# Weight splitting one attention step later, and attention's loads ahead of the weight pieces, in a fused attention and expert-layer kernel

## The chip, the cores and the metric

The kernel runs on one core of a Trainium2 chip. The metric is the device time of one execution in microseconds (us). The core has TensorE (PE, with its weight loads as PEld), VectorE (DVE), ScalarE (ACT), GpSimd (POOL) and SyncE (SP), which here only issues DMAs. Each engine runs its instructions in the order of the program; they meet through semaphores.

## What is computed

The reference runs three layers one after the other. The first is an attention over 2 batches and 8 heads of size 64: 512 local queries see the keys within 32 places of their own and 32 global keys, and 32 global queries see all 544 keys. Its 1088 rows of 512 go through a dense layer with a squared relu (512 to 2048 to 512), and then through a layer of 8 experts, where each row takes one expert.

```python
s_ll = np.where(np.abs(pos[:, None] - pos[None, :]) <= 32, scale * q_l @ k_l.T, -1e9)
a_l = sm(np.concatenate([scale * q_l @ k_g.T, s_ll], axis=-1))
out_l = a_l @ np.concatenate([v_g, v_l], axis=2)
out_g = sm(scale * q_g @ k_all.T) @ v_all
x = concatenate([out_g, out_l], axis=2)          # rows of 512
x = np.square(np.maximum(x @ w_in, 0)) @ w_out   # moe_
# moe2_: expert e = argmax(x @ w_gate); out = gate * relu(x @ w1[e]) @ w2[e]
```

## The kernel before

**Attention** is a loop over steps u (line 248). A step handles half of a pair of heads: n = u // 2 is the pair (8 of them in the two batches), and 16 steps have scores; the loop runs on for a few more steps to drain its pipeline. What a step does, and in which order, stands in the string `ORDER`: `S0` and `S1` are the scores of the step's first and second two blocks (TensorE L123, VectorE L127 for mask and row minimum, ScalarE L130 for the exponential), `N` normalizes the step before (VectorE L134 and L135, GpSimd L138 and L140), `T` transposes the probabilities of two steps ago (TensorE L147 and L151, copied out by VectorE at L148 and by ScalarE at L152), `V0` and `V1` multiply the probabilities of three steps ago with the values (TensorE L165 and, for the global values, L168), `X` copies the result (ScalarE L175). Every fourth step also has the global queries: `GS` their scores (L186, L189), `GX` their maximum and exponential (VectorE L197 to L199, ScalarE L200 and L201), and in the three steps behind it `GN`, `GT` and `GV` (L206 to L234). Score tiles have two PSUM buffers (L60), which the global scores' second part uses too.

**Weights.** The next layer multiplies float32 numbers as sums of a high and a low part. `Weights` (line 283) makes these from pieces of 1 MB: `prefetch` loads a piece by DMA (L315) into one of three stage buffers, `queue` turns it into five steps, `last` (VectorE L359), `sign` (L364), `rebase` (ScalarE L367), `clamp` (VectorE L372) and `join` (L375), and the piece's end, `high` (ScalarE L336), `low` (VectorE L339) and the next `prefetch`, is hung on to steps of the piece behind it. `run(n)` issues the next n steps. The loop's places `f0` to `f4` call it: `EARLY[u][part]` is how many steps the place runs. The same places run the splits of x near the end of the loop (L511, L514).

**Loads.** `START` lists what is loaded ahead of the loop, `NEXT[n]` what is issued at `L` in the odd step of pair n, in this order, all on SP's queue: `k` keys and queries (L74, L75), `v` values (L80), `h` global values (L88), `g` global queries (L84), `w` pieces of weights (L315). SP runs them one behind the other, each with its waits: for its buffer, and for the load eight places earlier, whose semaphore it takes over. Keys have four buffers, queries three, values four, global queries one.

```python
for what in ORDER.split():
    if what == "S0" and u < NU: scores(u); scores_h(u, 0)
    ...
    elif what == "L" and hf == LH and n < len(NEXT):
        begin(NEXT[n])
    elif what[0] == "f":
        filler(u, int(what[1:]))      # W.run(EARLY[u][part])
```

Behind the loop come the dense layer (`moe1`: L533 to L535 and L553 to L555, with the rest of the weight steps among its matmuls) and the experts (`moe2`).

Of the kernel before, what the change touches and what calls it, by code (L numbers as in the profile page):

```python
# [22 lines left out]
LP, LV, GT, GV = 2, 3, 1, 2  # L23
NP, NPT = 3, 3
NS, CUT, NK, NQ, NV = 2, (0, 2, 4, 8), 4, 3, 4
START = "k1 v0 h w1 g0"
NEXT = ["w1 k2 v1", "w1 k3 v2", "k4 v3", "k5 v4 h0 h1", "k6 v5 g1 h2", "k7 v6 h3", "v7"]
LH = 1

SPLIT = [s for u in (16, 17, 18, 19) for s in ((u, 4), (u + 1, 2))]  # L30

EARLY = [[0] * 5] * 2 + [[1, 0, 1, 0, 0]] * 12 + [[0, 0, 1, 0, 0]] * 4 + [[0] * 5] * 4
RATE = [[2, 2]] * 8 + [[2, 3]] * 4 + [[0, 0]] * 4
RATE2 = [[0, 0]] * 8 + [[2, 3], [2, 2]] * 4
NST = 3
# [10 lines left out]
def attention(tc, ctx, ident, x, qb_d, kd_d, vw_d, qg_d, vg_d, filler):  # L46
# [175 lines left out]
    def g_pv(g):  # L222
        b = g // 2
        d = gs.pop(("t", g))
        o = ps_o.tile([128, 4, 64], F32, name="og", tag="o")
        for j in range(2):
            v = ld["v", 2 * g + j]
            for c in range(5):
                k, w = (slice(0, 128), 2 * c) if c < 4 else (slice(64, 96), 7)
                for h in range(2):  # L230
                    p, q = slice(64 * h, 64 * h + 64), slice(64 * j + 32 * h, 64 * j + 32 * h + 32)
                    nc.tensor.matmul(o[p, j, 0:32], lhsT=v[k, w, p], rhs=d[k, c, q], start=(c == 0), stop=(c == 4))
        hp0 = 2 * g % 4
        nc.vector.tensor_copy(x[:, hp0:hp0 + 2, b * ST:b * ST + SG], o[:, 0:2, 0:32])  # L234

    def begin(what):
        for w in what.split():
            if w[0] == "w":
                filler(-1, int(w[1:]))
            elif w == "h":  # L240
                load_vg(0, slice(0, 512))
            elif w[0] == "h":
                load_vg(1, slice(128 * int(w[1:]), 128 * int(w[1:]) + 128))
            else:
                {"k": load, "v": load_v, "g": load_g}[w[0]](int(w[1:]))

    begin(START)
    for u in range(NU + LV + 2):
        n, hf = divmod(u, 2)
        g, r = divmod(u, 4)  # L250
        for what in ORDER.split():
# [23 lines left out]
            elif what == "GV" and r == GV and 0 < g <= 4:  # L275
                g_pv(g - 1)
# [3 lines that stand above are left out]
# [125 lines left out]
def attention_moe_kernel(ctx, tc, qb, kd, vw, qg, vg, w_in, w_out, w_gate, w_gate_t, w1, w2, capacity, out):  # L405
# [24 lines left out]
    def filler(u, part):  # L430
        if u < 0:
            W.prefetch(part)
        else:
            W.run(EARLY[u][part])
        for v, p in SPLIT:
# [684 lines left out]
```

## Time and profile before

| | |
|---|---|
| time, median of 3 runs (lowest to highest) | 462.59 us (462.2 to 468.64) |
| the profiled execution: its time, its span | 462.7 us, 461.0 us |
| PE busy | 432.4 us (94%) |
| DVE, ACT, POOL busy | 315.8 us (69%), 249.1 us (54%), 79.4 us (17%) |
| mean granted clock of PE | 0.988 |
| moved by DMA | 77.26 MB, mean 168 GB/s |
| attention's loop | up to 85.56 us, the first matmul of the dense layer |

The span runs from the first to the last instruction. A row of a timeline has the start in us, the length, the engine, the line, what is written and read, and in brackets how long the engine had been idle before it and what ended that. A row of a wait has the total, how many times, and the longest. The granted clock of 1.00 is 2.4 GHz, 0.50 is 1.2 GHz. A matmul of float32 numbers is two instructions in the rows.

### The profile page before, as it was taken

The numbers are of one execution on the slowest core, as the hardware profiler recorded it, in microseconds if no ns is written. First come the engines' busy times: TensorE is split into PE (matmuls) and PEld (weight loads), VectorE is DVE, ScalarE is ACT, GpSimd is POOL, SyncE is SP. The second block draws the span as 40 slices with busy tenths as digits, with TensorE's granted clock in tenths as the row PEclk, the third lists the DMA queues.
The fourth block names the chain that finished last, engine by engine and source line by source line (L and its number), as shares of the span: only waits on it lengthen the run. The fifth ranks groups of instructions, "written<-read, shape, count | busy, mean of one in ns | idle before, by whom it ended". The sixth has DMA issues, their size and how long they took to land. (4 is left out here: it accounts for less than half of the span.)

```text
span 461.0 us, 8010 instructions
## 1 busy us (share of the span) xinstructions
PE 432.4 (94%) x2963; PEld 368.8 (80%) x2963; DVE 315.8 (69%) x690; ACT 249.1 (54%) x488; POOL 79.4 (17%) x106
## 2 busy tenths in 40 slices
PE   5799999999999999999999999799999999999992
PEld 4677777888887889899999999677787777877970
DVE  3598987588799627974598688466974888647200
ACT  4587876576777734222533393156755777356210
POOL 3265636000000000000000000403202512051010
PEclk9899999999999999999999999899999999999998
DMA  8958952325254421005010468485992899711010
GB/s 250 399 182 316 326 196 94 96 91 182 97 186 176 169 104 48 24 1 194 25 46 1 146 254 332 122 257 208 306 305 95 309 349 366 298 52 41 1 39 21
DMA packets 24601, 77.26 MB, mean 168 GB/s; under 512 B 3689, under 2 KB 4841, under 8 KB 24288
## 3 DMA queue, kind: packets, MB, share of 16 engines
q1 hardware_dynamic: 19456, 64.38, 38.7%
q0 software_dynamic: 2384, 6.78, 4.9%
q10 hardware_dynamic: 2704, 5.37, 3.2%
q8 instruction: 32, 0.52, 0.5%
q14 instruction: 25, 0.20, 0.1%
HBM read 70.08 MB, written 7.41 MB: 168 GB/s over the span
## 5 line engine op out<-in xcount | busy, mean ns | idle before, releaser
L339 DVE TENSOR_TENSOR wlo<-ws,whi 128x1024 fp32r<-128x1024 f32 x80 | 94.6, 1219 | 11.5 <-ACT whi L336 10.5
L336 ACT CAST whi<-ws 128x1024 fp32r<-128x1024 f32 x80 | 83.0, 1075 | 19.2 <-DVE ws L375 10.3
L554 PE MATMUL y<-gl,whi 128*128 128x512 f32 (+2 forms) x192 | 63.2, 329 | 1.6 <-DVE gl L545 1.6
L533 PE MATMUL h<-xh,whi 128*128 128x512 f32 (+2 forms) x192 | 63.8, 332 | 0.6 <-ACT r L539 0.6
L535 PE MATMUL h<-xh,wlo 128*128 128x512 f32 (+2 forms) x192 | 62.9, 328 | 0.2 <-DVE wlo L339 0.2
L553 PE MATMUL y<-gh,whi 128*128 128x512 f32 (+2 forms) x192 | 62.9, 327 | 0.0
L534 PE MATMUL h<-xl,whi 128*128 128x512 f32 (+2 forms) x192 | 62.8, 327 | 0.0
L555 PE MATMUL y<-gh,wlo 128*128 128x512 f32 (+2 forms) x192 | 62.8, 327 | 0.0
L539 ACT ACTIVATE r<-h 128x512 f32<-128x512 f32 (+2 forms) x48 | 22.5, 470 | 42.8 <-PE h L535 35.7
L554 PEld LDWEIGHTS y<-gl,whi 128*128 128x128 f32 x192 | 36.3, 189 | 4.8 <-DVE gl L545 2.3
L533 PEld LDWEIGHTS h<-xh,whi 128*128 128x128 f32 x192 | 36.3, 189 | 3.4 <-ACT r L539 0.9
L535 PEld LDWEIGHTS h<-xh,wlo 128*128 128x128 f32 x192 | 36.3, 189 | 3.1 <-DVE wlo L339 0.6
L534 PEld LDWEIGHTS h<-xl,whi 128*128 128x128 f32 x192 | 36.3, 189 | 2.5
L545 DVE TENSOR_TENSOR gl<-r,gh 128x512 fp32r<-128x512 f32 (+2 forms) x48 | 25.7, 536 | 18.4 <-ACT r L542 15.5
L553 PEld LDWEIGHTS y<-gh,whi 128*128 128x128 f32 x192 | 36.3, 189 | 2.5
L555 PEld LDWEIGHTS y<-gh,wlo 128*128 128x128 f32 x192 | 36.3, 189 | 2.5
L130 ACT ACTIVATE P<-P,mn 128x160 f32<-128x160 f32 x64 | 27.0, 427 | 16.4 <-DVE mn L127 14.1
L583 DVE CUSTOM_DVE_ANT_0 junk<-yr,ws 128x512 bf16<-128x512 f32 x48 | 33.1, 690 | 1.2
L123 PE MATMUL s<-kd,qb 128*128 128x160 f32 x128 | 26.7, 343 | 5.2 <-DMA qb<-qb 5.2
L904 PE MATMUL bank_o<-whi,hh 128*128 128x512 f32 x72 | 29.9, 415 | 0.0
L870 POOL DMA_INDIRECT out_dram<-os,sidx x11 | 12.6, 1145 | 97.1 <-ACT os L866 96.5
L905 PE MATMUL bank_o<-wlo,hh 128*128 128x512 f32 x72 | 28.3, 393 | 0.0
(205 smaller groups left out, 895.0 us busy)
## 6 DMA issues: line engine op xcount, KB each, us to landing
ws<-w SPq DMA_DIRECT2D x62, 512.0 KB
ws<-w_in SPq DMA_DIRECT2D x8, 1024.0 KB
ws<-w_out SPq DMA_DIRECT2D x8, 1024.0 KB
vw<-vw SPq DMA_DIRECT2D x8, 512.0 KB
qb<-qb SPq DMA_DIRECT2D x7, 512.0 KB
kd<-kd SPq DMA_DIRECT2D x7, 416.0 KB
ws<-w_gate_t SPq DMA_DIRECT2D x2, 1024.0 KB
out_dram<-yr ACTq DMA_DIRECT2D x1, 2048.0 KB
```

What stands on the lines that cost most here:

```text
L130: nc.scalar.activation(out=P[:, a], in_=P[:, a], func=AF.Exp, bias=mn[:, a:a + 1], scale=-1.0, accum_out=su[:, a:a + 1])
L336: self.nc.scalar.copy(d["h"], f)
L339: self.nc.vector.tensor_tensor(out=d["l"], in0=f, in1=d["h"].bitcast(F32), op=ALU.subtract)
L533: nc.tensor.matmul(h, lhsT=whi[:, k, fs], rhs=xh[k], start=(k == 0), stop=False)
L534: nc.tensor.matmul(h, lhsT=whi[:, k, fs], rhs=xl[k], start=False, stop=False)
L535: nc.tensor.matmul(h, lhsT=wlo[:, k, fs], rhs=xh[k], start=False, stop=(k == 3))
L553: nc.tensor.matmul(ys[d][:, 0:gh.shape[1]], lhsT=whi[:, f % 4, ds_], rhs=gh, start=(f == 0), stop=False)
L554: nc.tensor.matmul(ys[d][:, 0:gh.shape[1]], lhsT=whi[:, f % 4, ds_], rhs=gl, start=False, stop=False)
L555: nc.tensor.matmul(ys[d][:, 0:gh.shape[1]], lhsT=wlo[:, f % 4, ds_], rhs=gh, start=False, stop=(f == 15))
L583: nc.vector.tensor_tensor_reduce(out=junk, in0=yr, in1=wgb[e], scale=1.0, scalar=0.0, op0=ALU.mult, op1=ALU.add, accum_out=L[:, i, e:e + 1])
L904: nc.tensor.matmul(o, lhsT=hh[:, k], rhs=wh[:, k % 4], start=(k == 0), stop=False)
L905: nc.tensor.matmul(o, lhsT=hh[:, k], rhs=wl[:, k % 4], start=False, stop=False)
```

## The change

Three tables of numbers and words are changed, no function.

```diff
-START = "k1 v0 h w1 g0"
-NEXT = ["w1 k2 v1", "w1 k3 v2", "k4 v3", "k5 v4 h0 h1", "k6 v5 g1 h2", "k7 v6 h3", "v7"]
+START = "k1 v0 h g0 w1"
+NEXT = ["k2 v1 w1", "k3 v2 w1", "k4 v3", "g1 k5 v4 h0 h1", "k6 v5 h2", "k7 v6 h3", "v7"]
-EARLY = [[0] * 5] * 2 + [[1, 0, 1, 0, 0]] * 12 + [[0, 0, 1, 0, 0]] * 4 + [[0] * 5] * 4
+EARLY = [[0] * 5] * 3 + [[1, 0, 1, 0, 0]] * 12 + [[0, 0, 1, 0, 0]] * 4 + [[0] * 5] * 3
```

By `EARLY` the weight steps begin in u=3 instead of u=2, and each of the 28 steps of the loop stands one u later. By `START` and `NEXT` the global queries stand ahead of the first piece, the keys, queries and values of pairs 2 and 3 ahead of the second and third piece, and the second batch's global queries are loaded in u=7 instead of u=9.

On VectorE, from the normalization in u=2 on, in the kernel before (`ws` is the piece of weights, `tp` the transposes, `PT` their copy, `P` the probabilities):

```order
L135 RECIPROCAL su<-su 128x4
L359 TENSOR_SCALAR ws<-ws 128x1024
L148 COPY PT<-tp_239 128x128
L127 ISA P,mn<-s,mask 128x160
L127 ISA mn 128x1
...
L364 SCALAR_TENSOR_TENSOR ws<-ws 128x1024
```

and from the same place in the changed one, to the same step of weights:

```order
L135 RECIPROCAL su<-su 128x4
L148 COPY PT<-tp_238 128x128
L127 ISA P,mn<-s,mask 128x160
L127 ISA mn 128x1
...
L135 RECIPROCAL su<-su 128x4
L359 TENSOR_SCALAR ws<-ws 128x1024
L148 COPY PT<-tp_282 128x128
...
L364 SCALAR_TENSOR_TENSOR ws<-ws 128x1024
L197 TENSOR_REDUCE m_306<-sg 128x1
```

The first weight step L359 moved from ahead of the first copy of transposes to ahead of the second one, and L364 to just ahead of the maximum of the first global scores.

On ScalarE, from the exponentials of u=2 and u=3 on, in the kernel before:

```order
L130 ACTIVATE P,su<-P,mn 128x160 x4
L367 ACTIVATE ws<-ws 128x1024
L152 COPY PT<-tp 128x512
L130 ACTIVATE P,su<-P,mn 128x160 x2
L200 ACTIVATE Pg,sg__310<-sg,nbg 128x480
L201 ACTIVATE Pg,sg__310<-sg_303,nbg 128x64
L175 COPY x<-o 128x256
```

and in the changed one:

```order
L130 ACTIVATE P,su<-P,mn 128x160 x4
L152 COPY PT<-tp 128x512
L130 ACTIVATE P,su<-P,mn 128x160 x2
L200 ACTIVATE Pg,sg__308<-sg,nbg 128x480
L201 ACTIVATE Pg,sg__308<-sg_301,nbg 128x64
L175 COPY x<-o 128x256
L130 ACTIVATE P,su<-P,mn 128x160 x2
L367 ACTIVATE ws<-ws 128x1024
L152 COPY PT<-tp 128x512
```

The rescaling L367 moved from ahead of the copy of transposes in u=3 to ahead of the copy in u=4.

On SP, at the beginning of its loads, as one piece of the difference (`kd` keys, `qb` queries, `vw` values, `vgz` global values, `qg` global queries):

```order
 L80 DMA vw<-vw 128x1024
 L88 DMA vgz<-vg 32x512 x4
+L84 DMA qg<-qg 128x512
 L315 DMA ws<-w_in 128x2x1024
-L84 DMA qg<-qg 128x512
+L74 DMA kd<-kd 128x832
+L75 DMA qb<-qb 128x1024
+L80 DMA vw<-vw 128x1024
 L315 DMA ws<-w_in 128x2x1024
 L74 DMA kd<-kd 128x832
```

The global queries moved ahead of the first piece, and the keys, queries and values of pair 2 ahead of the second.

## Rows read from the trace of the kernel before

**Rows 1.** Windows: length; busy us (count) of PE, PEld, DVE, ACT, POOL; PEclk, DMA.

```profile
22.35:40.61 18.26, 17.62 (x238) 14.19 (x234) 16.25 (x61) 14.60 (x48) 11.55 (x12) 1.00 0.70 268
...
85.56:290.00 204.44, 201.41 (x1263) 184.30 (x1259) 155.06 (x328) 102.79 (x175) 0.53 (x1) 1.00 0.34 121
290.00:461.00 171.00, 156.07 (x772) 123.66 (x772) 96.59 (x126) 84.96 (x118) 37.44 (x32) 0.98 0.53 185
```

**Rows 2.** Waits of PE up to 22.35 us: total, times, longest.

```profile
PE o L168 <- DVE PT L148: 2.3, 1, 2.3
```

**Rows 3.** Timeline of DVE, where weight steps begin.

```profile
15.59 0.69 DVE L359 TENSOR_SCALAR ws<-ws 128x1024 int32<-128x1024 int32 x1 [3.22 <-DMA ws<-w_in]
16.20 0.28 DVE L148 COPY PT<-tp 128x128 f32<-128x128 f32 x1
16.41 0.31 DVE L127 CUSTOM_DVE_ANT_0 P<-s,mask 128x160 f32<-128x160 f32 x1
...
16.89 1.22 DVE L364 SCALAR_TENSOR_TENSOR ws<-ws 128x1024 int32<-128x1024 int32 x1
```

**Rows 4.** Timeline of PE: steps 3, 4 and 5, and step 7 into 8.

```profile
13.87 0.34 PE L165 MATMUL o<-PT,vw 128*64 128x64 f32 x4
16.54 0.48 PE L168 MATMUL o<-PT,vgz 128*64 128x64 f32 x4 [2.34 <-DVE PT L148]
...
18.50 1.20 PE L123 MATMUL s<-kd,qb 128*128 128x160 f32 x4
...
22.35 0.81 PE L123 MATMUL s<-kd,qb 128*128 128x160 f32 x4
...
24.31 0.71 PE L123 MATMUL s<-kd,qb 128*128 128x160 f32 x4
...
26.31 0.34 PE L165 MATMUL o<-PT,vw 128*64 128x64 f32 x4
...
36.03 0.34 PE L165 MATMUL o<-PT,vw 128*64 128x64 f32 x4
...
37.24 0.71 PE L123 MATMUL s<-kd,qb 128*128 128x160 f32 x4
...
40.61 0.81 PE L123 MATMUL s<-kd,qb 128*128 128x160 f32 x4
```

**Rows 5.** Windows at the start, columns as in rows 1; the last two: DMA share, GB/s.

```profile
0.00:15.50 15.50, 8.87 (x37) 7.50 (x37) 5.17 (x25) 6.53 (x22) 5.95 (x21) 1.00 0.86 283
...
12.50:14.50 2.00, 1.71 (x14) 1.39 (x13) 0.00 (x0) 0.89 (x3) 1.54 (x3) 1.00 1.02 405
...
16.40:19.50 3.10, 2.96 (x21) 2.84 (x22) 2.63 (x13) 1.99 (x9) 0.47 (x2) 0.50 1.03 411
```

**Rows 6.** The page's DMA issues: what, queue, count, KB each.

```profile
ws<-w_in SPq DMA_DIRECT2D x8, 1024.0 KB
...
qg<-qg SPq DMA_DIRECT2D x2, 256.0 KB
```

**Rows 7.** Timelines of DVE and ACT, steps 3 and 4.

```profile
21.45 0.66 DVE L197 TENSOR_REDUCE m<-sg 128x1 f32<-128x480 f32 x1 [0.31 <-PE sg L186]
...
19.29 1.13 ACT L367 ACTIVATE ws<-ws 128x1024 f32<-128x1024 f32 x1
...
22.59 0.66 ACT L200 ACTIVATE Pg<-sg,nbg 128x480 f32<-128x480 f32 x1 [0.87 <-DVE nbg L199]
...
23.53 0.37 ACT L175 COPY x<-o 128x256 f32<-128x256 f32 x1
...
24.61 0.58 ACT L152 COPY PT<-tp 128x512 f32<-128x512 f32 x1
```

**Rows 8.** Waits of PE from 22.35 to 85.56 us.

```profile
PE tp L151 <- POOL Pw L140: 0.7, 2, 0.4
...
PE sg L186 <- DMA qg<-qg: 0.3, 1, 0.3
```

**Rows 9.** GpSimd's products: ns of one, shortest, median, longest.

```profile
L140 POOL TENSOR_TENSOR Pw<-P,su x32: 607/614/1692, 10.6 to 78.6; 128x256 f32<-128x256 f32 x32
```

## The prediction, made before the changed kernel was run

> **What bounds the kernel now.** I read four views in this order. The windows by stage [rows 1] tell who is full: in the first whole four steps of the attention loop (22.35 to 40.61 us) TensorE is busy 17.62 of 18.26 us and VectorE 16.25; from the dense layer on (85.56 to 290 us) TensorE is busy 201.41 of 204.44 us, in the last stage 156.07 of 171.00. So from 22 us on TensorE sets the pace, and what it gains before is carried to the end, unless it is lost again to a new wait. The waits of TensorE then tell where it stood still before 22 us [rows 2]: apart from the first loads, once, 2.3 us, for the copy at L148. The timeline of VectorE shows why [rows 3]: L359, the first split step of a weight piece, began at 15.59 after 3.22 us of waiting for its DMA, so VectorE had been free since 12.37; L148, which needs nothing of the weights, stood behind it and began at 16.20. TensorE's own timeline [rows 4] shows the hole: L165 at 13.87, L168 only at 16.54. The windows around it [rows 5] add the second half of the price: TensorE's granted clock was 1.00 (2.4 GHz) before the hole, and 0.50 (1.2 GHz) from 16.40 to 19.50 behind it.
>
> **What the change removes.** Steps of attention are called u. In u=2 VectorE no longer meets L359 and L364, so L148 can start at 12.37 and the hole in front of L168 goes. TensorE's work from the first L165 of a step to its second scores takes 1.21 us at full clock (36.03 to 37.24 in step 7), and from there to the next step's first scores, global scores included, 3.37 us (37.24 to 40.61) [rows 4]. So step 3's second scores come at 13.87 + 1.21 = 15.08 (before 18.50), step 4's first scores at 18.45 (before 22.35). Up to here TensorE gains 3.90 us: the hole and the slow clock.
>
> **What it puts in its place: VectorE's chain in step 3.** L359 now stands in step 3, and still waits for the first piece. That piece lies in the queue behind one more load, the global queries, of 256 KB [rows 6]. By 15.50 us the queue had moved 283 GB/s x 15.5 us = 4.4 MB [rows 5], while the loads up to and with the piece are 3.7 MB (416 + 512 KB twice for keys and queries, 512 for values, 256 for global values, 1024 for the piece, by the shapes in the code): so it went nearly in the order of issue, and 262 kB more at 405 GB/s is 0.65 us: landing at 16.24. Bounds: 15.59, if the queries cost nothing; and 15.59 + 0.65 + 3.6 = 19.9, if the piece shares the engines evenly with the keys, queries and values now issued behind it (416 + 512 + 512 KB = 1.47 MB, 3.6 us at 405 GB/s). I take 16.24, since the bytes moved speak for order.
> From there, by starts and durations in rows 3: L359 0.61, L148 0.21, two L127 0.48, L364 1.22: VectorE reaches L197 at 18.76. From L197 to the first exponential of the global scores 1.14 us, and 0.94 to the copy behind the second one (21.45, 22.59, 23.53) [rows 7]: 20.84. Only then is the score buffer free that step 4's second scores take (two buffers, L60). Without that wait they would come at 18.45 + 1.96 (22.35 to 24.31) = 20.41. So TensorE waits 0.43 us and the gain falls to 24.31 - 20.84 = 3.47.
>
> **ScalarE in step 4.** The rescaling L367 (1.13 us) now stands in front of step 4's copy of the transposes (L152), where before it stood in step 3. From the copy L175 to L152 took 1.08 us (23.53 to 24.61), L152 itself 0.58 [rows 7]: 20.84 + 1.08 + 1.13 + 0.58 = 23.63. TensorE needs that copy for step 5's L165, which would otherwise come 2.00 us after step 4's second scores (24.31 to 26.31 [rows 4]), at 22.84. It waits 0.79 us more: the gain falls to 26.31 - 23.63 = 2.68.
>
> **What it gives back later.** Two later waits of TensorE were for things that now come relatively earlier. In step 6 it waited 0.4 us for GpSimd's products L140 [rows 8]; with TensorE 2.7 us earlier and VectorE's sums (L134, L135) earlier by more than that (its chain above runs 3.4 to 4 us ahead of before), this wait goes: +0.4. In step 11 it waited 0.3 us for the second global queries [rows 8], whose load is now issued two steps earlier: +0.3. Sum: 2.68 + 0.4 + 0.3 = **3.4 us**.
>
> **What I cost at nothing.** The rest of the split steps only slide by one step: their number (28 before the dense layer) is the same, and two per step run against every phase of the four-step pattern in turn. The keys and queries of step 4 lie 1 MB earlier in the queue: 4.0 MB before them and 0.95 MB of their own, against 4.4 MB moved by 15.50, so the last byte at about 15.5 + 0.57/0.405 = 16.9 us, 1.5 us ahead of 18.45; the cover is thin, and a microsecond of lateness would be a microsecond of loss. The second load of global queries now waits, at SP, for the global scores of step 7, and the keys and values of step 10 stand behind it: about 37 us, for use about 46 us; nine us for some 2.5 MB. At the end of attention one split step more (L339, 1.2 us) and a rescaling lie among the splits of x; the capacity load behind them is later by about as much. TensorE's next needs there were covered by a few tenths, and I leave that as plus or minus 0.3.
>
> **The sum.** The profiled execution took 462.7 us (span 461.0), by 0.1 above the median of the three runs, 462.59. 462.7 - 3.4 = **459.3 us**.
>
> **The rivals.**
> 1. *A transfer takes the place of the wait.* The piece lands at 19.9, the late bound. VectorE's chain is then 3.7 us later, TensorE stands still in step 4 instead: 3.4 - 3.7 = -0.3, 463.0, no change that can be told; a fall of the clock in that new hole, as in the old one, would be 1.5 more. Against it: the bytes above. The Trainium skill ("DMA: Bandwidth & Descriptors", Queues, rings and completion order) says that completion is not in the order of issue over the 16 engines; by that rule this rival is open, and the 0.7 MB that had moved beyond the piece by 15.50 agree that the order is not strict. Chance 0.12.
> 2. *The clock falls all the same* (TensorE's work in steps 3 and 4 is not enough to hold it): 3.1 us at 0.50 [rows 5] cost half of that, 1.5 us: 460.8. Against it: in the walk above TensorE has no gap from 12.5 to 20.4 us. Chance 0.08.
> 3. *Slower: GpSimd becomes late.* One L140 took 607 to 1692 ns [rows 9], long where VectorE's split steps ran. If, with the steps one place on, the long ones fell into every step, TensorE would wait 0.4 us in each of the 14 steps from 2 to 15: 14 x 0.43 = 6.0 - 3.4 = 2.6 us slower, 465.3. It decides from 0.24 us a step on. Against it: it waited only twice [rows 8], and the products have a whole step (4.6 us, 18.26 / 4) before their transposes. The Trainium skill ("GPSIMD Engine Reference", Specifications) has GpSimd share its SBUF interfaces with VectorE, contended by VectorE instructions with two SBUF inputs; the 607 against 1692 ns agree. Chance 0.04.
> 4. *More gain*: neither the score buffer nor L367 holds TensorE (the piece lands at 15.59, and copies overlap better than in my walk): 3.90 + 0.7 = 4.6 us: 458.1. Chance 0.13.
>
> **How the numbers follow.** The forecast has 0.63, with its own range of 458.6 to 460.3. With rivals 2 and 4 that is 0.84: the range is 457.9 to 461.6, and leaves out rivals 1 and 3. A measurement of this kernel tells about 2% (9.3 us) from no change; the largest gain of any case is 4.6 us, the largest loss 2.6 us, so all of them lie within it: faster 0.01, same 0.98, slower 0.01.
>
> **What the profile of the changed kernel would show.** L148 first at about 12.4 and no wait of TensorE in front of the first L168; the granted clock 1.00 from 12.5 on; VectorE waiting about 1 us at the first L359, at 16.2; TensorE's first scores of step 4 at 18.5, second scores at 20.8 behind the global exponential, L165 of step 5 at 23.6 behind L152; no wait for the global queries in step 11; the first matmul of the dense layer at 85.56 - 3.4 = 82.2 us; stages behind that as long as before. The prediction is wrong if the first L359 begins after 17.2, if TensorE waits for a load of keys or queries after 10 us, or if the loop's four steps take over 18.5 us.

## The result and the profile after

Over 20 runs each, the changed kernel takes 460.45 us (median; 457.87 to 466.71) and the kernel before 464.88 us (462.2 to 469.32). The ratio is 0.9896, with a 95% interval of 0.9868 to 0.9925: a gain of 4.4 us by the medians and of 4.8 by the ratio (3.5 to 6.1), clear of the noise but inside the 2% that count as no change. Medians here are over all runs of a kernel; ratios, intervals and the last column of the table below leave out the few runs more than 1.5% above the kernel's fastest. The profiled execution took 462.06 us, with a span of 460.3 us. A second profile of the same kernel, from a run of its own (`after_again`, below), took 458.71 us, with a span of 457.0.

TensorE's timeline in the changed kernel, from the first L165 of step 3 to step 5 (start, length, engine, line, what; in brackets the idle time before and what ended it); it answers to [rows 4]:

```profile
15.60 0.34 PE L165 MATMUL o<-PT,vw 128*64 128x64 f32 x4
15.77 0.29 PE L168 MATMUL o<-PT,vgz 128*64 128x64 f32 x4
...
16.82 0.71 PE L123 MATMUL s<-kd,qb 128*128 128x160 f32 x4
...
20.18 0.81 PE L123 MATMUL s<-kd,qb 128*128 128x160 f32 x4
...
22.14 0.71 PE L123 MATMUL s<-kd,qb 128*128 128x160 f32 x4
...
24.88 0.34 PE L165 MATMUL o<-PT,vw 128*64 128x64 f32 x4 [0.68 <-ACT PT L152]
```

The first loads landed later in this execution, so step 3's first L165 comes at 15.60 where it stood at 13.87 [rows 4]. Counted from it, step 4's first scores follow after 20.18 - 15.60 = 4.58 us, before after 22.35 - 13.87 = 8.48: the 3.90 us of the prediction. The same place in the second profile:

```profile
13.52 0.34 PE L165 MATMUL o<-PT,vw 128*64 128x64 f32 x4
...
18.55 0.78 PE L123 MATMUL s<-kd,qb 128*128 128x160 f32 x4 [0.34 <-issue]
...
20.48 0.71 PE L123 MATMUL s<-kd,qb 128*128 128x160 f32 x4
...
21.73 0.81 PE L123 MATMUL s<-kd,qb 128*128 128x160 f32 x4
23.58 0.34 PE L165 MATMUL o<-PT,vw 128*64 128x64 f32 x4 [1.04 <-ACT PT L152]
```

Here the first loads landed as in the kernel before (13.52 against 13.87), so this profile can be laid beside [rows 4] without a shift. VectorE and ScalarE of this second profile, which answer to [rows 3] and [rows 7]:

```profile
12.46 0.26 DVE L148 COPY PT<-tp 128x128 f32<-128x128 f32 x1
...
16.16 0.88 DVE L359 TENSOR_SCALAR ws<-ws 128x1024 int32<-128x1024 int32 x1 [1.36 <-DMA ws<-w_in]
...
17.64 1.22 DVE L364 SCALAR_TENSOR_TENSOR ws<-ws 128x1024 int32<-128x1024 int32 x1
18.78 0.65 DVE L197 TENSOR_REDUCE m<-sg 128x1 f32<-128x480 f32 x1
```

```profile
19.90 0.66 ACT L200 ACTIVATE Pg<-sg,nbg 128x480 f32<-128x480 f32 x1 [1.46 <-DVE nbg L199]
...
20.55 0.31 ACT L201 ACTIVATE Pg<-sg,nbg 128x64 f32<-128x64 f32 x1
...
20.84 0.37 ACT L175 COPY x<-o 128x256 f32<-128x256 f32 x1
...
21.93 1.13 ACT L367 ACTIVATE ws<-ws 128x1024 f32<-128x1024 f32 x1
22.94 0.59 ACT L152 COPY PT<-tp 128x512 f32<-128x512 f32 x1
```

The copy L148 is done by 12.7 and no longer stands behind L359, which waits for its piece until 16.16. In the first profile the piece came later:

```profile
17.33 0.70 DVE L359 TENSOR_SCALAR ws<-ws 128x1024 int32<-128x1024 int32 x1 [0.45 <-DMA ws<-w_in]
```

The waits of TensorE up to 90 us in the first profile (total, times, longest) have none for GpSimd and none for the global queries, which [rows 8] had:

```profile
PE s L123 <- DMA qb<-qb: 7.0, 4, 3.7
PE o L165 <- ACT PT L152: 1.3, 3, 0.7
PE o L168 <- DVE PT L148: 0.5, 1, 0.5
```

The windows of the same profile that answer to [rows 1], same columns: attention's four steps, the dense layer to 290 us, the rest.

```profile
20.18:37.88 17.70, 17.02 (x237) 14.10 (x233) 16.05 (x60) 14.63 (x48) 9.68 (x12) 1.00 0.82 312
82.38:290.00 207.62, 203.49 (x1266) 186.20 (x1263) 156.84 (x336) 104.01 (x177) 1.14 (x2) 0.99 0.34 124
290.00:460.30 170.30, 156.82 (x770) 123.80 (x769) 94.92 (x118) 84.84 (x118) 36.82 (x31) 0.97 0.53 184
```

The loop's four steps take 17.70 us (18.26 before), the dense layer begins at 82.38 instead of 85.56, 3.18 us earlier; yet the span is only 0.7 us shorter. The rest was lost behind the dense layer, in the stretch around 290 us where the rows are routed to their experts. The window from 275 to 300 us, of the kernel before, of the changed one, and of its second profile, in this order:

```profile
275.00:300.00 25.00, 22.49 (x144) 19.60 (x142) 16.35 (x47) 8.06 (x16) 5.62 (x6) 0.93 0.66 228
```

```profile
275.00:300.00 25.00, 22.88 (x127) 19.19 (x126) 13.66 (x43) 7.02 (x13) 5.61 (x6) 0.80 0.63 205
```

```profile
275.00:300.00 25.00, 22.49 (x135) 18.79 (x134) 15.92 (x44) 9.24 (x16) 5.62 (x6) 0.93 0.69 216
```

The granted clock there was 0.93, 0.80 and 0.93, and from the first matmul of the router to the first of the experts it took 16.03, 18.31 and 16.01 us. The instructions there are the same, so I put that loss to the execution and not to the change: where the clock held as in the kernel before, the second profile keeps its whole gain of 461.0 - 457.0 = 4.0 us to the end.

The stages of every profile, from timelines and pages, in us. L165: first one of step 3. S0(4): step 4's first scores. Dense: first matmul of the dense layer. Tail: from the router's first matmul to the experts'. The median is that of all runs of the kernel; the last column is explained below the table.

| kernel | L165 | L165 to S0(4) | S0(4) to dense | dense | tail | span | median | at 0.985 |
|---|---|---|---|---|---|---|---|---|
| before | 13.87 | 8.48 | 63.21 | 85.56 | 16.03 | 461.0 | 463.8 to 465.8 | 463.5 to 464.0 |
| after | 15.60 | 4.58 | 62.20 | 82.38 | 18.31 | 460.3 | 460.45 | 460.4 |
| after_again | 13.52 | 5.03 | 63.04 | 81.59 | 16.01 | 457.0 | 459.07 | 460.2 |
| split_only | 14.65 | 6.81 | 64.28 | 85.74 | 19.21 | 465.6 | 466.6 | 465.5 |
| loads_only | 13.28 | 7.82 | 62.65 | 83.75 | 17.43 | 460.6 | 464.69 | 463.9 |
| w_first | 14.09 | 6.91 | 61.81 | 82.81 | 16.02 | 459.5 | 463.05 | 462.8 |
| g1_late | 14.42 | 4.58 | 66.57 | 85.57 | 17.48 | 462.4 | 465.06 | 463.4 |
| g1_late_again | 13.62 | 5.49 | 66.50 | 85.61 | 17.72 | 464.1 | 464.03 | 463.5 |
| g0_after | 13.31 | 5.49 | 61.75 | 80.55 | 20.33 | 461.9 | 459.21 | 459.6 |
| split_u4 | 14.29 | 4.59 | 64.58 | 83.46 | 19.19 | 464.6 | 463.51 | 463.4 |
| rescale_f1 | 14.34 | 4.68 | 62.42 | 81.44 | 17.21 | 461.5 | 460.55 | 460.7 |
| k7_early | 15.35 | 4.58 | 62.40 | 82.33 | 17.81 | 459.4 | 461.33 | 460.5 |
| filled | 14.48 | 7.03 | 62.74 | 84.25 | 16.11 | 459.7 | 463.93 | 464.1 |
| g1_filled | 13.56 | 4.95 | 65.05 | 83.56 | 16.00 | 460.3 | 462.92 | 463.4 |

The columns up to the dense layer are the ones to compare; the tail differs by up to 4.3 us between executions with the same instructions in it, and the span with it. It goes with the mean granted clock of the execution: 16.0 to 16.1 us in the five profiles with 0.988 to 0.991, 18.3 at 0.983 (`after`), 20.3 at 0.971 (`g0_after`).

The times go with it too. In every set of runs the time is longer where the mean granted clock of the run is lower, by 2.3 to 3.7 us per 0.01, on a straight line through the runs of one kernel. The last column reads each kernel's line at the same clock, 0.985. It is an estimate, and it also takes out a part of the clock that a kernel loses by its own holes. By it the change gains 3.1 to 3.8 us.

### The profile page after: what moved, and what is told of

Its sections match the earlier page's. It is cut to its first block, busy times and chain, and to the rows that moved or that the text cites. A ratio compares the mean times of both kernels' runs of the same rounds, so it can differ in the third digit from the quotient of the medians.

```text
span 460.3 us, 8006 instructions
## 1 busy us (share of the span) xinstructions
PE 433.2 (94%) x2963; PEld 370.1 (80%) x2963; DVE 316.7 (69%) x690; ACT 249.0 (54%) x488; POOL 78.4 (17%) x106
## 5 line engine op out<-in xcount | busy, mean ns | idle before, releaser
L339 DVE TENSOR_TENSOR wlo<-ws,whi 128x1024 fp32r<-128x1024 f32 x80 | 94.6, 1220 | 11.7 <-ACT whi L336 10.7
```

Of the source, the lines that this page charges most:

```text
L339: self.nc.vector.tensor_tensor(out=d["l"], in0=f, in1=d["h"].bitcast(F32), op=ALU.subtract)
```

## The experiments

**The splits alone, the loads alone.** The change has two halves. `split_only` takes only the table `EARLY` of the changed kernel:

```diff
-EARLY = [[0] * 5] * 2 + [[1, 0, 1, 0, 0]] * 12 + [[0, 0, 1, 0, 0]] * 4 + [[0] * 5] * 4
+EARLY = [[0] * 5] * 3 + [[1, 0, 1, 0, 0]] * 12 + [[0, 0, 1, 0, 0]] * 4 + [[0] * 5] * 3
```

> The split steps begin in u=3, the loads stand as before. Theory 'hole' (the gain is VectorE's copy L148 no longer standing behind L359, and the clock that stays up): no wait in front of the first L168, granted clock 1.00 from 12.5 to 20 us, and most of the gain, 2.5 to 4 us against the kernel before; what is missing to the full change is a wait of TensorE of 0 to 2 us at the first scores of step 4, whose keys and queries lie 1 MB later in the queue. Theory 'transfers' (the gain is the earlier keys and queries of pair 2 and the earlier global queries): TensorE stands 2 to 3 us at step 4 for the queries, and the kernel gains 0 to 1 us.

Measured: 466.6 us, ratio to the kernel before 1.0077 (1.0044 to 1.011): slower, which neither theory had. The hole at L168 is gone, as expected, but TensorE's timeline has two long waits, the one at step 4's first scores that both theories named, and one at the global scores of step 11 that neither did:

```profile
21.46 0.78 PE L123 MATMUL s<-kd,qb 128*128 128x160 f32 x4 [2.00 <-DMA qb<-qb]
```

```profile
56.54 1.99 PE L186 MATMUL sg<-kd,qg 128*128 128x512 f32 x4 [2.32 <-DMA qg<-qg]
```

The first is the mechanism of the prediction's rival 1, a transfer that takes the place of the wait, at another load: not the piece, but the queries behind it. `loads_only` takes the other half:

```diff
-START = "k1 v0 h w1 g0"
-NEXT = ["w1 k2 v1", "w1 k3 v2", "k4 v3", "k5 v4 h0 h1", "k6 v5 g1 h2", "k7 v6 h3", "v7"]
+START = "k1 v0 h g0 w1"
+NEXT = ["k2 v1 w1", "k3 v2 w1", "k4 v3", "g1 k5 v4 h0 h1", "k6 v5 h2", "k7 v6 h3", "v7"]
```

> The loads in the new order, the split steps from u=2 on as before. Theory 'hole': the first piece lands about 0.65 us later behind the global queries, L359 and so L168 wait 0.65 us longer, the clock falls to 0.50 as before: 0 to 1 us slower than the kernel before. Theory 'transfers': most of the gain is here, 2.5 to 4 us faster, although the hole in front of L168 is still there.

Measured: 464.69 us, ratio 1.0036 (1.0003 to 1.0069). The hole stays, and is longer, since the piece now lies behind the global queries. The clock behind it, against theory 'hole', stayed at 1.00:

```profile
16.64 0.34 PE L168 MATMUL o<-PT,vgz 128*64 128x64 f32 x4 [3.03 <-DVE PT L148]
17.74 0.71 PE L123 MATMUL s<-kd,qb 128*128 128x160 f32 x4
...
21.10 0.81 PE L123 MATMUL s<-kd,qb 128*128 128x160 f32 x4
```

So neither half gains anything; only together do they. The next three runs undo the loads one at a time, on one chip beside the changed kernel itself.

**The changed kernel again.**

> The changed kernel once more, on the chip of the next three, for a second profile and as their measure. If the change gives 3 to 4.5 us as the first comparison and the forecast have it: 0.989 to 0.993 of the kernel before, 460 to 461 us. In the profile, counted from the first L165 of step 3: step 4's first scores 4.5 to 4.7 us later (8.48 before), the first dense matmul 62.0 to 62.5 us behind those. If the shorter stretch was luck of one execution: 1.000 and counts that differ by more than 0.5 us.

Measured: 459.07 us, ratio 0.9871 (0.9821 to 0.9921). Time and ratio lie a little below what was expected; the runs of the kernel before beside it had a lower mean clock, 0.980 against 0.989. The first count missed its narrow range, 5.03 instead of 4.5 to 4.7, by the 0.34 us in front of step 4's first scores that the row above shows; the second, 63.04 instead of 62.0 to 62.5, has a wait of 0.97 us in step 14 in it, of which below. The gain itself stands.

**The pieces ahead of the keys again.**

```diff
-NEXT = ["k2 v1 w1", "k3 v2 w1", "k4 v3", "g1 k5 v4 h0 h1", "k6 v5 h2", "k7 v6 h3", "v7"]
+NEXT = ["w1 k2 v1", "w1 k3 v2", "k4 v3", "g1 k5 v4 h0 h1", "k6 v5 h2", "k7 v6 h3", "v7"]
```

> The changed kernel with the second and third piece of weights issued ahead of the keys, queries and values of pairs 2 and 3, as before the change. Theory A (order of the transfers): the queries of pair 2 land behind the second piece; TensorE waits about 2 us for them at step 4's first scores, which come 6.6 to 6.9 us behind step 3's first L165 (4.6 in the changed kernel); time 2 us above the changed kernel, 462.5. Theory B (the engines share the transfers, so order hardly counts): wait under 0.5 us, time within 0.5.

Measured: 463.05 us, ratio 0.9953 (0.991 to 0.9996), 4.0 us above the changed kernel beside it. The wait is there, and L165 to S0(4) takes 6.91 us, as theory A said:

```profile
21.00 0.78 PE L123 MATMUL s<-kd,qb 128*128 128x160 f32 x4 [2.26 <-DMA qb<-qb]
```

The price of 2 us is too small by the medians, and near at equal clock, 2.4 to 2.6 us. The profile gives 1.9 us more than `after_again` at step 4 and 2.3 more than `after`; at the dense layer 0.65 and 1.9 of them are left (82.81 - 14.09 = 68.72 us from L165, against 68.07 and 66.78).

**The second global queries late again.**

```diff
-NEXT = ["k2 v1 w1", "k3 v2 w1", "k4 v3", "g1 k5 v4 h0 h1", "k6 v5 h2", "k7 v6 h3", "v7"]
+NEXT = ["k2 v1 w1", "k3 v2 w1", "k4 v3", "k5 v4 h0 h1", "k6 v5 g1 h2", "k7 v6 h3", "v7"]
```

> The changed kernel with one load put back: the second batch's global queries again behind the values of pair 5, in u=9 instead of u=7. Theory A (order of SP's queue): the split steps stand one u later, so the piece's load ahead of the global queries in the queue waits one u longer for VectorE's last step of the piece before, and the queries land late. TensorE waits 1.8 to 2.3 us for them in step 11 as in the run that moved the splits alone, and the first dense matmul comes 64.0 to 64.5 us behind step 4's first scores (62.2 in the changed kernel); time 2 us above the changed kernel, 462.4. Theory B (the wait of that run came from its whole later chain): wait of 0.5 us or less, time within 0.5 of the changed kernel.

Measured: 465.06 us, ratio 1.0006 (0.9966 to 1.0045): with this one load of 256 KB in its old place, the changed kernel is no faster than the kernel before. TensorE's timeline in step 11:

```profile
51.74 0.71 PE L123 MATMUL s<-kd,qb 128*128 128x160 f32 x4
54.68 3.68 PE L186 MATMUL sg<-kd,qg 128*128 128x512 f32 x4 [2.23 <-DMA qg<-qg]
...
59.29 0.81 PE L123 MATMUL s<-kd,qb 128*128 128x160 f32 x4
```

and SP's queue ahead of it:

```profile
44.17 0.39 SPq L315 DMA_DIRECT2D ws<-w_in  x1
44.66 0.41 SPq L74 DMA_DIRECT2D kd<-kd  x1
45.12 0.42 SPq L75 DMA_DIRECT2D qb<-qb  x1
45.59 0.64 SPq L80 DMA_DIRECT2D vw<-vw  x1
46.34 0.55 SPq L84 DMA_DIRECT2D qg<-qg  x1
```

The prefetch L315 waits for VectorE's last step of the piece before,

```profile
42.95 1.19 DVE L339 TENSOR_TENSOR wlo<-ws,whi 128x1024 fp32r<-128x1024 f32 x1
```

which the change moves to one step of attention later; SP stood 3.3 us for it, until L339's end at 44.14. Behind it stand keys, queries, values and then the global queries, 2.7 MB with the piece. The same places in the kernel before:

```profile
45.72 0.39 SPq L315 DMA_DIRECT2D ws<-w_in  x1
...
47.97 0.59 SPq L84 DMA_DIRECT2D qg<-qg  x1
```

```profile
55.98 1.98 PE L186 MATMUL sg<-kd,qg 128*128 128x512 f32 x4 [0.31 <-DMA qg<-qg]
```

So the load did not become later in time. In the kernel before, SP came to this prefetch only after the loads of global values, at 45.62, when L339 had been over since 43.55, and the wait for the global queries ended at 55.98. In `g1_late` it ended 1.3 us earlier. But TensorE stood at L186 3.2 us earlier, at 52.45 instead of 55.67, and SP, which had got through the global values by 40.94, could not follow because L339 held it. That turns a wait of 0.3 us into one of 2.2. Theory A has the mechanism; the price it gave, 2 us, is half of the profile's: from S0(4) to the dense layer 66.57 us instead of 62.20 and 63.04, since the wait is followed by L186 at half clock. At equal clock it is 3.0 to 3.2 us. The windows in front of and behind it:

```profile
53.00:55.00 2.00, 0.32 (x1) 0.33 (x2) 1.63 (x5) 2.00 (x7) 2.00 (x2) 0.95 0.09 28
55.00:57.00 2.00, 2.00 (x3) 0.78 (x3) 0.00 (x0) 0.46 (x1) 0.11 (x1) 0.50 0.69 127
57.00:59.00 2.00, 2.00 (x16) 1.09 (x16) 0.61 (x2) 0.00 (x0) 0.00 (x0) 0.70 0.90 345
```

The two undone loads add up: 0.9953 and 1.0006 lie 0.8% and 1.35% above 0.9871, together 2.2%, and `split_only`, which has both (and the first global queries) undone, lies 1.8 to 2.1% above the changed kernel.

**The first global queries behind the first piece again.**

```diff
-START = "k1 v0 h g0 w1"
+START = "k1 v0 h w1 g0"
```

> The changed kernel with the first batch's global queries again behind the first piece. Theory A (the piece lands 0.65 us earlier, and the queries, needed 2 us later than the piece, still in time): 0 to 0.4 us faster than the changed kernel, VectorE without a wait at the first L359. Theory B (what the two loads of the runs above don't explain of the 6 us between the changed kernel and the one with only the splits moved lies here): 2 us slower, TensorE waiting for the global queries in step 3.

Measured: 459.21 us, ratio 0.9867 (0.9816 to 0.9918), as the changed kernel beside it (459.07). Of the load moves, this one did nothing that can be told: the piece came earlier (L359 at 15.20, and still with a wait, 0.66 us), and TensorE waited 0.6 us for the global queries, which theory A had in time. At equal clock these six runs are 0.6 to 0.8 us below the changed kernel, so the move of the first global queries is at least not shown to help.

**Is the hole's price the wait or the clock behind it?** Two kernels fill a hole with matmuls that nothing reads. The kernel before, filled at L168:

```diff
+            if u == 0 and a == 0:
+                z = ps_g.tile([128, 512], F32, name="z", tag="g")
+                for c in (416, 416, 416):
+                    nc.tensor.matmul(z[:, 0:c], lhsT=ident, rhs=ld["k", 0][:, 0:c], start=True, stop=True)
```

> The kernel before, with three extra matmuls of 416 columns (of the identity and the first keys, into a score tile that nothing reads) between the first L165 and the first L168 of step 3, about 2.3 us of work where TensorE stood still. They leave the wait for the copy at L148 as it is and only keep TensorE busy in it. Theory A (the hole's price has two halves, the wait and the clock behind it): L168 begins as late as before, but at a granted clock of 1.00, step 4's first scores come 4.4 to 4.5 us behind L168 (5.81 before), and the median falls by 1 to 1.4 us, ratio 0.997 to 0.998. Theory B (the slow clock behind the hole is rare in other executions, as in the one where only the loads were moved): ratio 1.000, within 0.4 us.

The lines of this kernel are 4 higher from here on (L168 is L172). Its timeline:

```profile
14.75 2.36 PE L169 MATMUL z<-kd,ident 128*128 128x416 f32 x6
17.04 0.34 PE L172 MATMUL o<-PT,vgz 128*64 128x64 f32 x4
...
21.51 0.81 PE L123 MATMUL s<-kd,qb 128*128 128x160 f32 x4
```

From L172 to step 4's scores it took 4.47 us, as theory A said (5.81 before [rows 4]), and the dense layer began at 84.25, 1.3 us earlier. But the median is 463.93 us, beside 463.79 of the kernel before, ratio 1.0005 (0.9971 to 1.004). So the slow clock behind the hole was in the execution profiled, and not a price that the usual execution can be shown to pay: the interval leaves no room for a gain over 1.3 us, though it doesn't exclude the low end of theory A. The clocks point to theory B: 3.1 us at half clock would take 0.0034 off the mean granted clock of a run (3.1 x 0.5 / 461), and the runs of `filled` have 0.9845 on average, those of the kernel before 0.9843, each good to about 0.002. `loads_only` says the same, with a hole of 3.03 us and the scores of step 4 only 4.46 us behind L168. The late global queries, filled:

```diff
+        if g == 2:
+            for c in (512, 512, 128):
+                nc.tensor.matmul(s[:, 0:c], lhsT=ident, rhs=ld["k", 4][:, 0:c], start=True, stop=True)
```

> The changed kernel with the second global queries loaded in u=9 once more, as the measure of the next one on the same chip. Expected as the first time: TensorE waits 2.0 to 2.5 us for them in step 11, then runs L186 at half clock, and the time is that of the kernel before, ratio 0.998 to 1.003, 4 to 6 us above the changed kernel. If the first 465.1 us were luck: 462 us.

> The same as the run ahead of it, with extra matmuls of 512, 512 and 128 columns (of the identity and keys, into the score tile that L186 then overwrites) in front of step 11's L186, about 2.1 us, as long as TensorE's wait for the global queries there. Theory A (half of the price of that wait is the clock behind it): L186 begins as late, but takes 1.9 us instead of 3.7; 1.5 to 2.5 us faster than the run ahead of it. Theory B (the clock falls there in few executions; the price of the late load lies in the wait and in what queues behind it): within 0.7 us of it.

Measured: 464.03 us unfilled (ratio 0.9979, 0.9948 to 1.001), 462.92 filled (0.9987, 0.9955 to 1.002). In the profile, L186 (here L189) takes 1.98 us, where `g1_late` had 3.68 and `g1_late_again` 2.81, and the dense layer begins at 83.56 instead of 85.61:

```profile
52.03 2.10 PE L185 MATMUL sg<-kd,ident 128*128 128x512 f32 x6
54.39 1.98 PE L189 MATMUL sg<-kd,qg 128*128 128x512 f32 x4 [0.25 <-DMA qg<-qg]
```

As before: shown for the profiled execution (2.0 us), and in the times neither theory's can be told (1.1 us by the medians, nothing by the ratios, 0.1 at equal clock).

**Three further moves.** `split_u4` begins the splits yet another step later:

```diff
-EARLY = [[0] * 5] * 3 + [[1, 0, 1, 0, 0]] * 12 + [[0, 0, 1, 0, 0]] * 4 + [[0] * 5] * 3
+EARLY = [[0] * 5] * 4 + [[1, 0, 1, 0, 0]] * 12 + [[0, 0, 1, 0, 0]] * 4 + [[0] * 5] * 2
```

> As the changed kernel, with the split steps one step of attention later still, from u=4 on. Theory 'chain' (in the changed kernel VectorE's L359 and L364 ahead of the first global maximum, and ScalarE's L367 ahead of L152 in step 4, still cost TensorE 0.4 to 1.2 us): the wait for L152 at the first L165 of step 5 goes, and it is 0.5 to 1.2 us faster than the changed kernel, 4 to 6 us faster than the kernel before. Rival: the steps that are pushed to the end of attention (u=18 and 19, among the splits of x) hold the first matmuls of the dense layer by as much: no faster than the changed kernel, within 0.5 us of it.

Measured: 463.51 us, ratio 0.9989 (0.9957 to 1.0021): the gain is gone. The chain at step 5 is better (no wait for L152), but the prefetch in SP's queue now waits another step longer. It is issued at 35.91, only 1.4 us ahead of the queries, where the changed kernel has 5.4 us (31.55 and 36.92 in `after_again`), and the queries are late in step 10:

```profile
45.49 0.78 PE L123 MATMUL s<-kd,qb 128*128 128x160 f32 x4 [1.85 <-DMA qb<-qb]
```

The rival has a part in it as well: from the first matmul of the dense layer to the router's first it takes 199.72 us (83.46 to 283.18), in the two profiles of the changed kernel 198.12 and 197.87, and TensorE waits 1.2 us for the weight step L339 there, 0.2 and nothing in those two.

`rescale_f1` lets the second weight step of u=4 run behind the copy L152 instead of ahead of it, against the wait in step 5:

```diff
-EARLY = [[0] * 5] * 3 + [[1, 0, 1, 0, 0]] * 12 + [[0, 0, 1, 0, 0]] * 4 + [[0] * 5] * 3
+EARLY = [[0] * 5] * 3 + [[1, 0, 1, 0, 0]] + [[0, 1, 1, 0, 0]] + [[1, 0, 1, 0, 0]] * 10 + [[0, 0, 1, 0, 0]] * 4 + [[0] * 5] * 3
```

> As the changed kernel, but in step 4 the rescaling L367 runs behind the copy L152 on ScalarE, not ahead of it; all else in the same order. Theory 'chain': the wait of TensorE for L152 at the first L165 of step 5, 0.68 us in the changed kernel's profile, goes, and the time is 0.5 to 0.8 us below the changed kernel's. Rival: VectorE's clamp L372, which waits for L367 and now gets it 0.6 us later, holds the next scores instead: no faster than the changed kernel.

Measured: 460.55 us, ratio 0.9941 (0.9904 to 0.9977). The wait is gone and smaller ones came for it; from S0(4) to the dense layer it takes 62.42 us, with the wait 62.20 and 63.04. `k7_early` takes the wait of step 14 away, 0.31 us in the first profile of the changed kernel and this in the second:

```profile
63.05 0.78 PE L123 MATMUL s<-kd,qb 128*128 128x160 f32 x4 [0.97 <-DMA qb<-qb]
```

```diff
-NEXT = ["k2 v1 w1", "k3 v2 w1", "k4 v3", "g1 k5 v4 h0 h1", "k6 v5 h2", "k7 v6 h3", "v7"]
+NEXT = ["k2 v1 w1", "k3 v2 w1", "k4 v3", "g1 k5 v4 h0 h1", "k6 v5 h2 k7", "v6 h3", "v7"]
```

> The changed kernel with the keys and queries of pair 7 issued one pair earlier (u=9 instead of u=11), so that they no longer stand in SP's queue behind the prefetch of a piece that waits for VectorE. TensorE waited 0.31 and 0.97 us for them in step 14 in the two profiles of the changed kernel. Theory A: that wait goes and the dense layer begins 0.3 to 1 us earlier, counted from step 4's first scores (61.3 to 62.0 us); time 0.3 to 1 us below the changed kernel, ratio to before 0.985 to 0.989. Theory B (the wait hides others, which end just behind it, or the earlier load delays another one): no gain, or a new wait for queries or values between steps 9 and 12.

Measured: 461.33 us, ratio 0.9923 (0.9891 to 0.9955). Theory B: the wait went, one for GpSimd took its place, and the stretch is 62.40 us:

```profile
65.22 0.66 PE L151 MATMUL tp<-ident,Pw 128*128 128x128 f32 x4 [0.43 <-POOL Pw L140]
```

None of the three can be told to beat the changed kernel: at equal clock they lie at 463.4, 460.7 and 460.5 us, the changed kernel at 460.4 and 460.2. The gains looked for in the last two, under 1 us, are smaller than the intervals, so it is the profiles that speak there.

## Why the prediction was right, step by step

- **The hole goes, 3.90 us.** Right in place and size where the clock had fallen: 4.58 us from L165 to S0(4) after, 8.48 before. But 1.4 of the 3.90 (5.81 - 4.41 us from L168 on, 16.54 to 22.35 [rows 4] against 15.77 to 20.18) were the slow clock, and neither `filled` nor `loads_only` gives a sign that the usual execution of the kernel before pays it.
- **The piece lands at 16.24.** In the second profile L359 began at 16.16. In the first it began at 17.33, past the 17.2 that I had set as a sign of error; there all loads were later, and the wait at L359 was 0.45 us, shorter than the 1 us predicted, not longer. The mark should have been set from the first L165, not from the span's start.
- **The score buffer holds step 4's second scores until 20.84.** Wrong. Step 4's second scores, S1(4), began at 20.48 without a wait, while L201 still read its buffer until 20.86; of the two buffers, S1(4) therefore took the other one, and the one behind L201 went to the next scores, S0(5), which began at 21.73 without a wait. The walk of VectorE and ScalarE up to there was right (L197 at 18.78 for 18.76, the copy L175 at 20.84 for 20.84), only the instruction that waits was named wrongly. It cost the sum nothing, since the next wait ends later and swallows it.
- **L367 ahead of L152 makes step 5's L165 wait until 23.63.** It waited until 23.58 in the second profile, 1.04 us; in the first 0.68 us. Right.
- **The waits for GpSimd in step 6 and the global queries in step 11 go.** Both are gone.
- **Costed at nothing.** The sum survived, but by less cover than "nothing" says. The last byte of step 4's keys and queries was put at 16.9, 1.5 us ahead of need. In front of step 4's first scores the second profile has 0.34 us that it names only as issue; TensorE's queue sat at a semaphore there until 18.46, after VectorE's part (L127, to 17.7), so I take it for the keys or queries landing late, which is inferred. Two other profiles have the landing: the queries came 6.5 us after their issue at 12.48 in `g1_late_again` and 6.2 after 12.22 in `g1_filled`, so at 18.98 and 18.42, each 0.1 us before the first scores, which had stood 0.77 and 0.29 us. In these there was no cover at all: bytes moved, taken in the order of issue, gave a landing 1.5 to 2 us too early; the second global queries arrive in time only because they were moved (2.2 us otherwise); and I missed that the keys and queries of step 14 stand behind a prefetch that waits one step longer: 0.31 and 0.97 us. A wait for keys or queries after 10 us was one of my three signs of error, and it came.
- **The dense layer at 82.2.** 82.38 and 81.59.
- **The sum.** 459.3 us, against a median of 460.45: off by 1.2, inside the range of 457.9 to 461.6. That it is so near is partly luck: it started from a median of three runs, 462.59, where 20 runs have 464.88, 2.3 us more, and the gain from there was 4.4 (or 4.8) and not 3.4, so two misses took each other back in part. The profiles give 3.2 and 4.0 us at the dense layer, and the runs at equal clock 3.1 to 3.8, around the 3.4 predicted. So the rest of the medians' difference goes with the clocks that the runs happened to get. In the profiles the clock differs most in the routing stretch; why it falls there in some executions is open. How the gain divides is open too: 1.4 us of the hole's price were the slow clock, which was in one execution.
- **The rivals.** Rival 1's mechanism is real, at the queries behind the piece, and only the load half of the change keeps it away: 4 us by the median and 2.5 at equal clock where the pieces stand first. Rival 2 did not happen at steps 3 and 4 (the clock was 1.00 from L168 to S0(4) in every profile without a hole). Rival 3 did not: the loop's four steps were shorter than before. Rival 4's time, 458.1, is below the median, though its first half (no hold by the score buffer) is what happened.

## What to carry to other kernels

When work is moved forward, the loads it needs must be able to follow. Here TensorE came 3 to 4 us earlier, while its loads stood behind a large transfer, or behind a prefetch that waits for the very step that had been moved later; what the change gained was lost again until the loads were moved ahead of both. So go through the queue with every blocked issue, and ask for each load behind it when it is needed; a load of 256 KB in the wrong place cost most or all of the gain. A wait that is found in a profile of one execution is not yet a gain: of three that were taken away here, those of `rescale_f1` and `k7_early` only handed the time to the next wait. And where the times of one kernel follow the granted clock, compare kernels at the same clock before a difference of 1% is explained.

## What the runs showed of the hardware

- The clock behind a hole is not a fixed price. Behind the kernel before's hole of 2.34 us it was 0.50 [rows 4, 5], and behind those of 2.23 us in `g1_late` and 2.29 us in `g1_late_again` too; behind holes of 3.03 us (`loads_only`), 2.26 us (`w_first`) and 2.00 and 2.32 us (`split_only`) it stayed at 1.00. In the routing stretch the same instructions ran with a granted clock of 0.80 or 0.93 between 275 and 300 us, worth 2.3 us, in two executions of one kernel.
- A wait for a load can end a microsecond after the queue looks empty. The global queries in `g1_late` were issued at 46.34, and by 53.5 us the transfers had all but ended (0.06 and 0.04 of the engines' time, 25 and 12 GB/s in the next two half microseconds), but TensorE's wait for them ended only at 54.68. The Trainium skill ("DMA: Bandwidth & Descriptors", Queues, rings and completion order) has one copy split over up to 16 engines that finish independently of each other, and completion not first in, first out. The low share in that window agrees with a few late engines; which load its packets belong to, the rows don't say.
- GpSimd slows beside some of VectorE's steps. In the kernel before, one product L140 of 128x256 takes 0.61 us; the five that take 1.59 to 1.69 us each run beside an L339, L364 or L375 (at 30.4, 34.1, 38.5, 52.4 and 70.4 us).
- The first loads' landing scatters: the first L165 of step 3 came between 13.28 and 15.60 us in the profiles, without a relation to the order of the loads that these profiles show.
